# Float64 pairs in buffers of their own, x sums in eighths, an exponential unit in timed steps: a fused attention, expert and two-layer kernel

## The chip, the cores and the metric

One core of a Trainium2 chip runs the whole kernel. The metric is device time in microseconds (us). The engines are PE (TensorE: matmuls into PSUM), DVE (VectorE), ACT (ScalarE), POOL (GpSimd) and SP (SyncE), whose queue issues every DMA of this kernel, one after the other. Each engine runs its own instructions in the order in which the program emitted them; semaphores, placed by the tile framework, make an instruction wait for what it reads or overwrites.

## The reference

```python
attn = attention(q_l, k_l, v_l, q_g, k_g, v_g)        # 4 x 8 heads, 512 local (window 32) + 32 global rows
x = attn as 2176 rows of 512
P = exp(x @ w_gate - max); 8 times: rows, then columns of P divided by their sums     # 8 experts
x = sum over e of P[:, e] * (relu(x @ w1[e]) @ w2[e])   # w1: 512 x 1024, w2: 1024 x 512
h = x @ w_in                                            # 512 x 2048, float64 weights
g = where(h > 0, h, exp(min(h, 0)) - 1)                 # the exponential unit
out = g @ w_out                                         # 2048 x 512, float64 weights
```

## The kernel before, in words

Products are made in float32 accuracy: each operand is split into a high part hi (fp32r, a cast on ACT) and the remainder lo (a subtraction), and each product is three matmuls, hi x hi, hi x lo and lo x hi (`three`). The first layer of an expert or of the last network is computed with seven block products instead of eight (x and w in 2 x 2 blocks: sums t1 to t4 of w, s1 to s4 of x); `Quad.product(i)` makes one of them and, after it, `keep` (a partial sum s1, u2 or u3 in a `tmp` tile of that name, two buffers each) or `evac` (the result: the sum on DVE, then the activation into hh and hl, the two parts of the hidden layer in `hs`).

The stages follow each other: attention with the first two units in its gaps; then the MoE in two passes over the rows (pass 0: 1024 rows, 512-column products; pass 1: 1152 rows, 288-column products), 16 units of 512 hidden columns each; then the last network, called the second pass here, in 16 turns (turns 0 to 7 are its first 1024 rows, 8 to 15 the others, a tail ends them). `order` lists the MoE units from the third on: its units 0 to 13 are pass 0, 14 to 29 pass 1. A unit is `mix1` (first layer, two or four quads) and `mix2_all` (second layer: 8 or 9 tiles of 128 rows, each 12 matmuls into one PSUM bank, then `acc` on DVE).

All other work of the MoE stage is put between these steps by two lists of functions, written out by hand. `side1` is emptied in `mix1`, some functions after each product; `side2` in `mix2_all`, some after each tile. `None` in a list is a step in which nothing is emitted. In `side1` stand the loads of the next unit's w1 (w1r), the split of w2 into `w2s`, and the loads of other work; in `side2` the build of the next unit's w1 parts (`b1`: sums on POOL, hi on ACT, lo on DVE), `between` and `end` (other work) and the load of w2 (w2r). Loads go into four rotating `raw` tiles; a load waits until the tile's last use is over, and SP's later DMAs wait behind it.

The other work, by unit:
- `PAIRS`: `weights64_pair`. Two chunks of w_in (float64) are loaded; `words` takes the float32 value from the bits in six DVE instructions, with its results in ct and cp, which use the tags u2 and u3; `value` adds the rest (ACT, POOL). Then the four sums, hi and lo of seven blocks, in four further raw tiles, and 14 stores of 128 KB into scratch memory.
- singles (`weights64`): one chunk of w_out each, with hi and lo in `tmp` tiles (ch, cl) and two stores.
- `BACK`: `x_back`, the transposes of the first rows of the MoE's result.
- `OPERANDS`: `x_operands(2, c)`, two of four chunks of x: load, four sums on DVE (xsr), hi on ACT, lo on DVE, four stores; the chunks of the other rows (p = 3) run in turns 3 to 6.

In the second pass the order of a turn is a string: `a1` is product 1 of the turn's quad, `z3` product 3 of the quad before, `t4` the second layer's tile 4 (`part2`). `elu` computes the unit as max(t, 0) plus (e + 1) times the tanh of half of min(t, 0), with e its exponential: ACT makes three functions (relu, exp, tanh: tiles er and eg), DVE two instructions (the join, L1036 and L1037), ACT the cast hh, POOL the subtraction hl. What follows the three functions is a closure in `late`, which `rests()` runs at the next `elu` or at the end of the next `part2`. `passed(ns)` counts PE's work in `clock["now"]`; it served the gate's normalization only (`sinkhorn`).

Of the kernel before, what the change touches and what calls it, by code (L numbers as in the profile page):

```python
# [11 lines left out]
F32 = mybir.dt.float32  # L12
# [40 lines left out]
TURN_A = "a1 a6 t4 a2 t5 z3 t6 a7 t7 a5 t0 a4 t1 t2 t3"  # L53
# [8 lines left out]
def tile_net(ctx: ExitStack, tc, kq, vw, vc, qg, wg, w1, w2, wi, wo, consts, out):  # L62
# [721 lines left out]
    class Chunk:  # L784
# [9 lines left out]
        def words(self):  # L794
            top = self.r[:, :, 1]
            t = self.t = tmp.tile([128, 512], F32, tag="u2", name="ct")
            p = self.p = tmp.tile([128, 512], F32, tag="u3", name="cp")
# [7 lines left out]
            nc.vector.tensor_scalar(pi, ti, -2**23, None, op0=ALU.bitwise_and)  # L805

# [9 lines left out]
    def weights64(u, k):  # L816

        c = Chunk(wo[u, :, k])

        def parts():  # L820
            t = c.t
            hi = tmp.tile([128, 512], F32R, tag="s1", name="ch", bufs=2)
            lo = tmp.tile([128, 512], F32R, tag="cl", name="cl", bufs=1)
# [61 lines left out]
    def x_operands(p, c):  # L885

        k, g = divmod(c, 2)
        m = TP[p - 2] // 4
        s = {}

        def load():
            s["x"] = raw_tile((4, m), F32, "xr")
# [4 lines left out]
        def sums():  # L897
            x11, x21, x12, x22 = (s["x"][:, i] for i in range(4))
            t = s["s"] = raw_tile((4, m), F32, "xsr")
            s1, s2, s3, s4 = (t[:, i] for i in range(4))  # L900
            for o, a, b, op in (
                (s1, x21, x22, ALU.add), (s3, x11, x21, ALU.subtract), (s2, s1, x11, ALU.subtract), (s4, x12, s2, ALU.subtract),
            ):
                nc.vector.tensor_tensor(out=o, in0=a, in1=b, op=op)

        def hi(n):
            s[n + "h"] = raw_tile((4, m), F32R, "xh")
            nc.scalar.copy(s[n + "h"], s[n])

        def lo(n):  # L910
            nc.vector.tensor_tensor(out=s[n].bitcast(F32R), in0=s[n], in1=s[n + "h"].bitcast(F32), op=ALU.subtract)
            o = 0 if n == "x" else 4
            for q, t in (("h", s[n + "h"].bitcast(F32)), ("l", s[n])):
                nc.sync.dma_start(xo[p, q][:, o:o + 4, k, g * m:(g + 1) * m], t)

        return load, [sums, lambda: hi("x"), lambda: hi("s"), lambda: lo("x"), lambda: lo("s")]
# [18 lines left out]
    def sinkhorn():  # L935
# [62 lines left out]
    late = deque()  # L998
# [5 lines left out]
    class Quad:  # L1004
# [21 lines left out]
        def elu(self, hh, hl, t):  # L1026

            r = tmp.tile([128, 512], F32, tag="cl", name="er", bufs=1)[:, :self.n]
# [121 lines left out]
    with tc.manual_schedule():  # L1150
# [21 lines left out]
        back = {}  # L1172
# [99 lines left out]
        for k in range(len(turns) + 1):  # L1272
# [15 lines left out]
            for e in seq:  # L1288
# [8 lines left out]
                else:  # L1297
# [4 lines left out]
                    if i == 4 and q is quads[-1]:  # L1302
                        renew(k, W22[:-1])
# [79 lines left out]
```

## Time and profile before

| | us |
|---|---|
| median of 3 runs | 2113.37 (2111.77 to 2116.02) |
| the profiled execution | 2116.6 |
| its span, first to last instruction | 2114.8 |
| PE busy | 2020.4 |
| DVE busy | 1504.0 |
| ACT busy | 829.9 |
| POOL busy | 751.5 |
| mean granted TensorE clock | 0.981 |

The span is what the trace covers; the profiled execution's own time has 1.8 us around it. A granted clock of 1 is 2.4 GHz, 0.5 is 1.2 GHz. A windows row gives a stretch's length, then busy us and instruction count of PE, PEld (weight loads), DVE, ACT and POOL, the granted clock, the DMA engines' busy share and GB/s. Timeline rows are start, duration, engine, line, operation, out<-in and, in brackets, the engine's idle time before it with what ended it.

### The profile page before, as it was taken

The numbers are of one execution on the slowest core, as the hardware profiler recorded it, in microseconds if no ns is written. First come the engines' busy times: TensorE is split into PE (matmuls) and PEld (weight loads), VectorE is DVE, ScalarE is ACT, GpSimd is POOL, SyncE is SP. The second block draws the span as 40 slices with busy tenths as digits, with TensorE's granted clock in tenths as the row PEclk, the third lists the DMA queues.
The fourth block names the chain that finished last, engine by engine and source line by source line (L and its number), as shares of the span: only waits on it lengthen the run. The fifth ranks groups of instructions, "written<-read, shape, count | busy, mean of one in ns | idle before, by whom it ended". The sixth has DMA issues, their size and how long they took to land. (4 is left out here: it accounts for less than half of the span.)

```text
span 2114.8 us, 30653 instructions
## 1 busy us (share of the span) xinstructions
PE 2020.4 (96%) x11099; PEld 1740.5 (82%) x11099; DVE 1504.0 (71%) x2833; ACT 829.9 (39%) x1672; POOL 751.5 (36%) x649
## 2 busy tenths in 40 slices
PE   9999999999999999999999999999999998899998
PEld 8998888888888877798888888988889876678776
DVE  7767676677767777667676777878888566666666
ACT  6655424233233333333333333333333254445554
POOL 6656322233223355224242424444444121222221
PEclk9999999999999999999999999999999999899999
DMA  7446351132232233822324243232232945664321
GB/s 233 132 132 211 90 203 50 54 112 72 97 110 83 82 95 95 311 90 87 98 85 146 88 150 95 80 95 80 85 110 85 278 148 188 193 226 122 109 90 65
DMA packets 201047, 262.16 MB, mean 124 GB/s; under 512 B 13760, under 2 KB 147136, under 8 KB 200896
## 3 DMA queue, kind: packets, MB, share of 16 engines
q1 hardware_dynamic: 200896, 260.21, 38.6%
q8 instruction: 87, 1.43, 0.3%
q14 instruction: 64, 0.52, 0.1%
HBM read 194.62 MB, written 65.54 MB: 123 GB/s over the span
## 5 line engine op out<-in xcount | busy, mean ns | idle before, releaser
L133 PE MATMUL m<-w2h,hh 128*128 128x512 f32 x1360 | 542.6, 399 | 30.4 <-ACT hh L1038 24.9
L137 PE MATMUL m<-w2h,hl 128*128 128x512 f32 x1360 | 542.3, 399 | 15.2 <-POOL hl L1039 10.8
L135 PE MATMUL m<-w2l,hh 128*128 128x512 f32 x1360 | 539.1, 396 | 1.5 <-POOL w2l L129 1.5
L1020 ACT ACTIVATE hh<-t 128x288 fp32r<-128x288 f32 (+1 forms) x368 | 184.7, 502 | 432.1 <-DVE t L1014 429.5
L133 PEld LDWEIGHTS m<-w2h,hh 128*128 128x128 f32 x1360 | 259.2, 191 | 89.3 <-ACT hh L1038 34.1
L137 PEld LDWEIGHTS m<-w2h,hl 128*128 128x128 f32 x1360 | 258.6, 190 | 81.5 <-POOL hl L1039 24.3
L135 PEld LDWEIGHTS m<-w2l,hh 128*128 128x128 f32 x1360 | 259.0, 190 | 53.3 <-POOL w2l L129 4.2
L129 POOL TENSOR_TENSOR w2l<-w2r,w2h 128x512 fp32r<-128x512 f32 x120 | 163.0, 1380 | 388.9 <-ACT w2h L125 374.1
L1022 DVE SCALAR_TENSOR_TENSOR hl<-t,hh 128x288 fp32r<-128x288 f32 (+1 forms) x368 | 274.4, 746 | 28.0 <-ACT hh L1020 24.4
L1108 DVE SCALAR_TENSOR_TENSOR acc<-m,pr,acc 128x512 f32<-128x512 f32 x247 | 182.8, 745 | 117.9 <-PE m L137 116.5
L1039 POOL TENSOR_TENSOR hl<-eg,hh 128x288 fp32r<-128x288 f32 (+1 forms) x96 | 94.3, 982 | 362.7 <-ACT hh L1038 269.6
L1014 DVE TENSOR_TENSOR t<-q,u 128x288 f32<-128x288 f32 (+1 forms) x348 | 182.9, 526 | 52.3 <-PE q L1067 44.4
L741 POOL TENSOR_TENSOR wt<-w1r,wt 128x512 f32<-128x512 f32 x60 | 88.0, 1467 | 180.1 <-DVE hl L1022 94.3
L745 ACT CAST wh<-wt 128x512 fp32r<-128x512 f32 x120 | 69.9, 618 | 206.9 <-POOL wt L741 206.9
L741 POOL TENSOR_TENSOR wt<-w1r 128x512 f32<-128x512 f32 x60 | 79.8, 1334 | 181.4 <-DVE hl L1022 133.9
L1048 DVE TENSOR_TENSOR u<-q,s 128x288 f32<-128x288 f32 (+1 forms) x116 | 61.2, 528 | 98.0 <-PE q L1067 50.8
L749 DVE TENSOR_TENSOR wl<-wt,wh 128x512 fp32r<-128x512 f32 x120 | 121.8, 1032 | 2.2 <-ACT wh L745 1.0
L1036 DVE SCALAR_TENSOR_TENSOR eg<-eg,er 128x288 f32<-128x288 f32 (+1 forms) x96 | 51.7, 538 | 95.2 <-ACT er L1032 95.1
L1046 ACT COPY s<-q 128x288 f32<-128x288 f32 (+1 forms) x116 | 51.9, 448 | 114.6 <-PE q L1067 93.8
L1038 ACT CAST hh<-eg 128x288 fp32r<-128x288 f32 (+1 forms) x96 | 47.5, 495 | 117.8 <-DVE eg L1037 117.8
L810 POOL TENSOR_TENSOR cp<-r,cp 128x512 f32<-128x512 f32 x32 | 48.4, 1511 | 127.4 <-ACT r L809 78.3
L1249 DVE TENSOR_TENSOR acc<-m,acc 128x512 f32<-128x512 f32 x119 | 80.6, 683 | 17.3 <-PE m L137 17.3
(241 smaller groups left out, 4760.7 us busy)
## 6 DMA issues: line engine op xcount, KB each, us to landing
w1r<-in_w_dram SPq DMA_DIRECT2D x60, 512.0 KB, 6.4
w2r<-in_w_dram SPq DMA_DIRECT2D x60, 512.0 KB, 5.3
kq<-in_kq_dram SPq DMA_DIRECT2D x31, 544.0 KB, 4.2
wh<-wqh SPq DMA_DIRECT2D x98, 128.0 KB, 3.0
wl<-wql SPq DMA_DIRECT2D x98, 128.0 KB, 2.9
r<-in_wo_dram SPq DMA_DIRECT2D x16, 512.0 KB, 4.0
r<-in_wi_dram SPq DMA_DIRECT2D x16, 512.0 KB, 3.9
vw<-in_vw_dram SPq DMA_DIRECT2D x32, 227.5 KB, 4.7
```

Of the source, the lines that this page charges most:

```text
L129: e.tensor_tensor(out=lo, in0=src, in1=hi.bitcast(F32), op=ALU.subtract)
L133: nc.tensor.matmul(ps, ah, bh, start=first, stop=False)
L135: nc.tensor.matmul(ps, ah, bl, start=False, stop=False)
L137: nc.tensor.matmul(ps, al, bh, start=False, stop=last)
L741: eng.tensor_tensor(out=t, in0=get(a), in1=get(b), op=op)
L749: eng.tensor_tensor(out=wop[n + "l"], in0=src, in1=wop[n + "h"].bitcast(F32), op=ALU.subtract)
L1014: nc.vector.tensor_tensor(out=t, in0=ps, in1=rest, op=ALU.add)
L1020: nc.scalar.activation(hh, t, AF.Relu)
L1022: late.append(lambda: nc.vector.scalar_tensor_tensor(out=hl, in0=t, scalar=0.0, in1=hh.bitcast(F32), op0=ALU.max, op1=ALU.subtract))
L1039: nc.gpsimd.tensor_tensor(out=hl, in0=g, in1=hh.bitcast(F32), op=ALU.subtract)
L1108: nc.vector.scalar_tensor_tensor(out=accs[i], in0=ps, scalar=scale, in1=accs[i], op0=ALU.mult, op1=ALU.add)
L1249: nc.vector.tensor_tensor(out=accs[i], in0=ps, in1=accs[i], op=ALU.add)
```

## The change

- `PAIRS` move from units 10, 11, 12, 15, 17, 19, 21, 23 to 16, 18, 20, 22, 24, 26, 27, 28. Singles stand one each in units 1, 2, 4, 6, 8, 10, 11, 12, and two each in 17, 19, 21, 23 (before: one in 2, 4, 6, 8; two in 22 and 24 to 28). `BACK` is 14 and 15.
- ct and cp use the tags eg and cl, two buffers each. A pair's further results go into its two loaded tiles (`room`), into ct and into cp, and no longer into four raw tiles; its lo's move to POOL. Sums stand inside `b1`, the first casts (`plain`) in `end`; `hi`, `lo` and `store` become `later`, the first functions of the next unit's `side1`. A single's hi goes into its loaded tile, after `rest`, its lo into cp.
- x chunks become eight of half the width, sums in the loaded tile, lo on POOL, two stores. In pass 1 they stand in units 17, 19, 21, 23 (one each) and 25 (four). From unit 16 on `side2` is b1, end, between, w2r loads; before it was b1, between, w2r loads, end. In the second pass the loads are emitted one turn ahead (turns 2 to 5), the rest in turns 3 to 6.
- `elu` puts a join and a parts step into `stages`, due 1700 + 1.8 n ns and a further 500 + 1.5 n ns of counted PE time later (n columns); each is run after the first product or tile at which the clock is there, or at an `elu` that finds two units open. `part2` counts its matmuls. t0 stands behind a4 in `TURN_A`.

```diff
-BACK = (14, 16)
-OPERANDS = (18, 20)
-PAIRS = (10, 11, 12, 15, 17, 19, 21, 23)
+BACK = (14, 15)
+OPERANDS = {17: 1, 19: 1, 21: 1, 23: 1, 25: 4}
+PAIRS = (16, 18, 20, 22, 24, 26, 27, 28)
-TURN_A = "a1 a6 t4 a2 t5 z3 t6 a7 t7 a5 t0 a4 t1 t2 t3"
+TURN_A = "a1 a6 t4 a2 t5 z3 t6 a7 t7 a5 a4 t0 t1 t2 t3"
...
-            t = self.t = tmp.tile([128, 512], F32, tag="u2", name="ct")
-            p = self.p = tmp.tile([128, 512], F32, tag="u3", name="cp")
+            t = self.t = tmp.tile([128, 512], F32, tag="eg", name="ct", bufs=2)
+            p = self.p = tmp.tile([128, 512], F32, tag="cl", name="cp", bufs=2)
...
+        def room(self, dt, n=1):
+            r = self.r.rearrange("p f w -> p (f w)").bitcast(dt)
+            return r.rearrange("p (a f) -> p a f", a=n)
...
         def parts():
-            nc.scalar.copy(hi, t)
             c.rest()
-            nc.gpsimd.tensor_tensor(out=t, in0=t, in1=hi.bitcast(F32), op=ALU.subtract)
-            nc.gpsimd.tensor_tensor(out=lo, in0=t, in1=c.p, op=ALU.add)
+            hi = c.room(F32R, 2)[:, 0]
+            nc.scalar.copy(hi, c.t)
+            nc.gpsimd.tensor_tensor(out=c.t, in0=c.t, in1=hi.bitcast(F32), op=ALU.subtract)
+            nc.gpsimd.tensor_tensor(out=c.p.bitcast(F32R), in0=c.t, in1=c.p, op=ALU.add)
...
         def plain():
+            nc.scalar.copy(c1.p.bitcast(F32R), c1.t)
+            nc.scalar.copy(c0.p[:, :256].bitcast(F32R), blk("11"))
         def hi():
+            nc.scalar.copy(c1.room(F32R, 4), c0.room(F32, 4))
         def lo():
+            for t, h in ((c1.t, c1.p), (blk("11"), c0.p[:, :256]), (c0.room(F32, 4), c1.room(F32, 4))):
+                nc.gpsimd.tensor_tensor(out=t.bitcast(F32R), in0=t, in1=h, op=ALU.subtract)
...
     def x_operands(p, c):
-        k, g = divmod(c, 2)
-        m = TP[p - 2] // 4
+        k, g = divmod(c, 4)
+        m = TP[p - 2] // 8
...
+        def lo(o):
+            x, h = s["x"][:, o:o + 4], s["h"][:, o:o + 4]
+            nc.gpsimd.tensor_tensor(out=x.bitcast(F32R), in0=x, in1=h.bitcast(F32), op=ALU.subtract)
+            if o:
+                for q, t in (("h", s["h"].bitcast(F32)), ("l", s["x"])):
+                    nc.sync.dma_start(xo[p, q][:, :, k, g * m:(g + 1) * m], t)
+        return load, [first, lambda: hi(0), second, lambda: lo(0), lambda: hi(4), lambda: lo(4)]
...
         def elu(self, hh, hl, t):
+            while sum(e[2] for e in stages) > 1:
+                stages.pop(0)[1]()
             ...
-            rests()
-            late.append(rest)
+            wait = 1700.0 + self.n * 1.8
+            stages.extend([(clock["now"] + wait, join, 0), (clock["now"] + wait + 500.0 + self.n * 1.5, parts, 1)])
+            stages.sort(key=lambda e: e[0])
...
             elif a in PAIRS:
-                lds, (w0, v0, w1_, v1), between = weights64_pair(*pairs.popleft())
+                lds, (w0, v0, w1_, v1), (*tail, lo, store) = weights64_pair(*pairs.popleft())
                 side1.extend(lds)
-                b1[17:17], b1[13:13], b1[9:9], b1[5:5] = [v1], [w1_], [v0], [w0]
+                b1[13:13], b1[11:11], b1[9:9], b1[6:6], b1[3:3] = [tail[0]], [v1], [w1_], [v0], [w0]
+                end, later = tail[1:2], [tail[2], lo, store]
...
+            for _ in range(OPERANDS.get(a, 0)):
+                ld, ops = chunks2.popleft()
+                between += [ld, None, None, None] + ops
...
-            side2.extend(b1 + between + ld2 + end)
+            side2.extend(b1 + end + between + ld2 if a > BACK[-1] else b1 + between + ld2 + end)
...
-                    pass
+                    passed(227.0)
...
-            if 3 <= k < 7:
-                ld, ops = x_operands(3, k - 3)
-                ops = [ld, None, None] + ops
+            if k == 2:
+                work = [x_operands(3, c) for c in range(8)]
+                ops = [None] * 8
+            elif 3 <= k < 7:
+                ops = work[2 * k - 6][1] + work[2 * k - 5][1]
+            if 2 <= k < 6:
+                ops += [work[2 * k - 4][0], work[2 * k - 3][0]]
...
+                while stages and clock["now"] >= stages[0][0]:
+                    stages.pop(0)[1]()
```

## Rows read from the trace of the kernel before

**Rows 1.** the page: busy us of each engine, its share, its instructions.
```profile
PE 2020.4 (96%) x11099; PEld 1740.5 (82%) x11099; DVE 1504.0 (71%) x2833; ACT 829.9 (39%) x1672; POOL 751.5 (36%) x649
```

**Rows 2.** windows of pass 0 (stretch, length, busy us, clock): units 10, 11-13.
```profile
704.30:745.20 40.90, 40.90 (x181) 33.75 (x180) 30.32 (x43) 13.20 (x23) 16.38 (x12) 1.00 0.24 78
745.20:886.80 141.60, 132.64 (x541) 105.41 (x540) 100.34 (x137) 44.58 (x79) 67.52 (x54) 0.94 0.50 170
```

**Rows 3.** windows of pass 1: units 15, 16, 18, 19, 20 to 24.
```profile
935.50:982.30 46.80, 46.80 (x278) 42.53 (x277) 38.40 (x67) 16.43 (x36) 18.39 (x13) 1.00 0.17 59
982.30:1037.50 55.20, 50.57 (x293) 45.32 (x292) 32.30 (x59) 17.30 (x37) 16.19 (x15) 0.97 0.39 118
1084.30:1138.30 54.00, 49.32 (x278) 44.22 (x277) 34.76 (x63) 17.21 (x35) 16.57 (x15) 0.97 0.37 119
1138.30:1189.10 50.80, 47.38 (x277) 42.60 (x276) 41.90 (x75) 18.26 (x38) 18.72 (x13) 1.00 0.37 118
1189.10:1446.00 256.90, 244.09 (x1382) 220.07 (x1382) 196.89 (x343) 87.18 (x181) 102.98 (x80) 0.97 0.35 111
```

**Rows 4.** windows of the second pass: turns 0-1, 2, 3-6, 7, 8 on.
```profile
1680.00:1719.90 39.90, 36.19 (x164) 29.29 (x163) 24.19 (x33) 22.22 (x38) 9.07 (x7) 0.91 0.59 175
1719.90:1742.00 22.10, 21.26 (x92) 16.72 (x91) 12.50 (x19) 10.37 (x17) 3.87 (x3) 1.00 0.55 166
1742.00:1856.60 114.60, 96.40 (x361) 73.27 (x360) 75.09 (x112) 49.72 (x76) 21.81 (x16) 0.90 0.61 191
1856.60:1880.20 23.60, 21.92 (x92) 16.60 (x91) 14.37 (x22) 11.12 (x19) 5.27 (x5) 1.00 0.93 334
1880.20:2110.60 230.40, 212.60 (x1159) 179.45 (x1157) 147.88 (x310) 120.61 (x278) 54.28 (x66) 0.99 0.32 99
```

**Rows 5.** waits of DVE in unit 11: total us, times, longest.
```profile
DVE u L1048 <- issue: 5.7, 1, 5.7
```

**Rows 6.** timeline of SP, unit 16: start, us, engine, line, operation.
```profile
985.73 1.43 SPq L870 DMA_DIRECT2D wqh<-wth  x3
...
994.58 0.97 SPq L778 DMA_DIRECT2D w2r<-in_w_dram  x2
```

**Rows 7.** timeline of ACT, unit 16 (in brackets the idle time before).
```profile
999.63 0.62 ACT L125 CAST w2h<-w2r 128x512 fp32r<-128x512 f32 x1 [5.94 <-DMA w2r<-in_w_dram]
```

**Rows 8.** timeline of SP at the end of unit 18.
```profile
1134.37 0.88 SPq L914 DMA_DIRECT2D xo2l<-xsr  x1
1135.36 2.54 SPq L895 DMA_DIRECT2D xr<-xe  x2
```

**Rows 9.** timeline of DVE around the end of unit 18.
```profile
1141.66 0.76 DVE L904 TENSOR_TENSOR xsr<-xr 128x256 f32<-128x256 f32 x2 [7.32 <-DMA xr<-xe]
...
1147.38 0.45 DVE L1048 TENSOR_TENSOR u<-q,s 128x288 f32<-128x288 f32 x1
```

**Rows 10.** waits of all engines from 1680 us on.
```profile
DVE eg L1036 <- ACT er L1032: 95.1, 80, 2.5
...
PE m L133 <- ACT hh L1038: 24.9, 22, 4.2
...
PE m L137 <- POOL hl L1039: 10.8, 25, 1.0
```

**Rows 11.** timeline of DVE in turn 4.
```profile
1779.40 0.83 DVE L904 TENSOR_TENSOR xsr<-xr 128x288 f32<-128x288 f32 x2 [3.06 <-DMA xr<-xe]
```

**Rows 12.** timeline of POOL at the end of unit 24.
```profile
1443.61 1.51 POOL L810 TENSOR_TENSOR cp<-r,cp 128x512 f32<-128x512 f32 x1 [3.18 <-ACT r L809]
1445.09 1.74 POOL L826 TENSOR_TENSOR ct<-ct,ch 128x512 f32<-128x512 f32 x1
1446.92 1.62 POOL L827 TENSOR_TENSOR cl<-ct,cp 128x512 fp32r<-128x512 f32 x1
```

**Rows 13.** timeline of DVE at the end of unit 24.
```profile
1442.28 0.43 DVE L805 TENSOR_SCALAR cp<-ct 128x512 int32<-128x512 int32 x1
```

**Rows 14.** groups of ACT, turns 0 to 7: count, busy us, mean ns.
```profile
L1031 ACT ACTIVATE eg<-er 128x512 f32<-128x512 f32 x31 | 19.6, 632 | 3.6 <-POOL hl L1039 1.0
```

**Rows 15.** timeline of DVE in unit 16.
```profile
1003.02 1.59 DVE L1022 SCALAR_TENSOR_TENSOR hl<-t,hh 128x288 fp32r<-128x288 f32 x1
...
1007.64 0.45 DVE L1022 SCALAR_TENSOR_TENSOR hl<-t,hh 128x288 fp32r<-128x288 f32 x1
```

**Rows 16.** timeline of POOL in unit 16.
```profile
1000.33 5.42 POOL L129 TENSOR_TENSOR w2l<-w2r,w2h 128x512 fp32r<-128x512 f32 x4 [12.65 <-ACT w2h L125]
```

More of the change, by code (lines that the diff above doesn't have):

```diff
@@ L841, in sums @@
         def sums():
-            t = s["t"] = raw_tile((4, 256), F32, "wt")
-            t1, t3, t4, t2 = (t[:, i] for i in range(4))
+            t1, t3, t4, t2 = (c0.room(F32, 4)[:, i] for i in range(4))
             for o, a, b in (
@@ L895, in load, with comb, first, second @@
                 nc.sync.dma_start(s["x"][:, 2 * a:2 * a + 2], src[:, k, a, :, g * m:(g + 1) * m])
[L897 to L916, printed above, removed]
+        def comb(o, a, b, op):
+            x = s["x"]
+            nc.vector.tensor_tensor(out=x[:, o], in0=x[:, a], in1=x[:, b], op=op)
+        def first():
+            comb(4, 1, 3, ALU.add)
+            comb(6, 0, 1, ALU.subtract)
+        def second():
+            comb(5, 4, 0, ALU.subtract)
+            comb(7, 2, 5, ALU.subtract)
+        def hi(o):
+            if o == 0:
+                s["h"] = raw_tile((8, m), F32R, "xh")
+            nc.scalar.copy(s["h"][:, o:o + 4], s["x"][:, o:o + 4])
+        def lo(o):
[5 more added lines that the diff above has]
+        return load, [first, lambda: hi(0), second, lambda: lo(0), lambda: hi(4), lambda: lo(4)]
     def operands(p, names, c0, c1):
@@ L941, in gmax @@
             nc.vector.tensor_reduce(out=mx, in_=lg.rearrange("p t e -> p (t e)"), axis=AX.X, op=ALU.max)
-            mb = sm.tile([128, 128], F32, tag="mb", name="mb")
+            mb = tmp.tile([128, 512], F32, tag="t", name="mb", bufs=3)[:, :128]
             nc.vector.tensor_copy(mb, mx.to_broadcast([128, 128]))
@@ L996, in passed @@
                 clock["due"] = clock["now"] + timed[0][0]
-    late = deque()
+    late, stages = deque(), []
     def rests():
@@ L1171, in tile_net @@
         singles = deque((u, k) for u in range(U2) for k in range(4))
-        back = {}
+        chunks2 = deque(x_operands(2, c) for c in range(8))
+        back, later = {}, []
         def load_back(j):
@@ L1186, in tile_net @@
             b1, ld2, load2 = [], [], nbuild
+            side1.extend(later)
+            later = []
             if moe:
@@ L1199, in tile_net @@
                 between = [lambda i=i: x_back(i) for i in range(2 * j, 2 * j + 4)]
-            elif a in OPERANDS:
-                lds, ops = zip(*(x_operands(2, 2 * OPERANDS.index(a) + c) for c in range(2)))
-                side1.append(lds[0])
-                between = [*ops[0], lds[1], *ops[1]]
             elif a in PAIRS:
-                lds, (w0, v0, w1_, v1), between = weights64_pair(*pairs.popleft())
+                lds, (w0, v0, w1_, v1), (*tail, lo, store) = weights64_pair(*pairs.popleft())
                 side1.extend(lds)
-                b1[17:17], b1[13:13], b1[9:9], b1[5:5] = [v1], [w1_], [v0], [w0]
-            elif not switch and a > 1 and singles:
-                if a < BACK[0]:
-                    ld, end = weights64(*singles.popleft())
-                    side1.append(ld)
-                else:
-                    (l0, (c0, d0)), (l1, (c1, d1)) = (weights64(*singles.popleft()) for _ in range(2))
-                    side1.extend([l0, l1])
-                    b1[13:13], b1[9:9], b1[5:5] = [c1], [d0], [c0]
-                    end = [d1]
+                b1[13:13], b1[11:11], b1[9:9], b1[6:6], b1[3:3] = [tail[0]], [v1], [w1_], [v0], [w0]
+                end, later = tail[1:2], [tail[2], lo, store]
+            elif a > 0 and not switch and len(singles) > 8:
+                ld, end = weights64(*singles.popleft())
+                side1.append(ld)
+            elif a > BACK[-1] and singles and OPERANDS.get(a) == 1:
+                (l0, (c0, d0)), (l1, (c1, d1)) = (weights64(*singles.popleft()) for _ in range(2))
+                side1.extend([l0, l1])
+                b1[13:13], b1[9:9], b1[5:5] = [c1], [d0], [c0]
+                end = [d1]
+            for _ in range(OPERANDS.get(a, 0)):
+                ld, ops = chunks2.popleft()
+                between += [ld, None, None, None] + ops
             if not moe:
@@ L1307, in tile_net @@
             prev = quads[-1] if quads else None
-        rests()
     mright.close()
```

34 lines of the change are left out of this document (8 added, 26 removed).

## The prediction

> **What bounds the kernel now.** I read the page's busy shares first: PE is busy 96% of the span, DVE, the busiest of the engines beside it, 71% [rows 1]. So what can be won is PE's idle time and its slow stretches, and the question is where they lie. The windows view tells, cut where a unit begins (the first product with x11 after a run of mix2 matmuls; unit a is the a-th of `order`). In pass 0 a clean unit takes 40.9 us, so its 180 matmuls of 512 columns stand 0.227 us apart. Pairs are built in units 10, 11 and 12, and the units 11 to 13 behind them take 141.6 us, 18.9 over three clean ones, at a granted clock of 0.94 [rows 2]. In pass 1 a clean unit takes 46.8 us (a 288-column matmul: (46.8 - 108 x 0.227) / 168 = 0.133). Seven units are longer: 16, 18, 20, 22 and 24, each behind a pair, and 19 and 21, each behind two operand chunks. With 23, which is clean, they make 16 and 18 to 24. These take 55.2 + 54.0 + 50.8 + 256.9 us, 42.5 over eight clean ones [rows 3]; 0.9 of it are the 16 transposes of unit 16 (a quarter of 0.227 each), so 41.6 can go: 4.0 in unit 19, as much taken for unit 21, and 33.6 behind pairs. The second pass (from 1680 us) needs 28.6 + 2.0 us for turns 0 and 1 (126 matmuls, 36 transposes), 90 x 0.227 = 20.4 for each of turns 2 to 7, and 672 x 0.133 + 486 x 0.227 = 199.5 for the rest. It takes 39.9, 22.1, 114.6 (turns 3 to 6), 23.6 and 230.4: over by 9.3, 1.7, 33.0, 3.2 and 30.9, together 78.1 [rows 4]. So 18.9 + 41.6 + 78.1 = 138.6 us can go.
>
> The waits then say why. Behind a pair in pass 0, DVE waits 5.7 us at `keep`, where u2 shares its two buffers with the pair's ct [rows 5]. In pass 1 the pair's 14 stores hold SP's queue for 8.8 us and w2r is issued behind them [rows 6]; ACT stands 5.94 us before the cast of w2r, with every relu behind it [rows 7]. Behind chunks, the load of the second is issued behind the stores of the first [rows 8], and DVE stands 7.32 us before its sums [rows 9]. In the second pass PE waits 24.9 us for hh and 10.8 for hl, and behind that is DVE's order: it stands 95.1 us in 80 places before the first instruction of the join for ACT's tanh, with the next t's and acc's queued behind [rows 10], and in turns 3 to 6 also for the x load, 3.06 us in one [rows 11].
>
> **The change, part by part** (each sum against the profiled execution, 2116.6 us, which is 3.2 above the median of 2113.4).
>
> *Pass 0 without pairs: -18.9.* Units 10 to 12 get a single each, as units 2 to 8 had. The new single keeps hi in the loaded tile, so ACT's copy now waits for POOL's multiplication of 1.5 us [rows 12]; it stands at the end of mix2, where ACT has nothing for PE. ct and cp no longer take u2 and u3. Bounds: 0 to 1 us lost per single.
>
> *Pairs in pass 1: -33.6 + 1.* w2r is now loaded before the stores, which move into mix1 of the next unit; there they stand before w1r, needed half a unit later. POOL does the pair's lo there, which slows DVE's hl (below); 0 to 1 us per pair, I take 1 for all eight.
>
> *One chunk behind two singles, units 17, 19, 21, 23: +22.* Here I see a new wait: the load of x follows the second single's stores on SP. Take unit 24, which has two singles and ends at 1446.0. The second single's words end at 1442.7 on DVE [rows 13]; multiplication 1.5, ACT's copy 0.6 (a cast of 512 columns, [rows 7]), subtraction 1.7 and addition 1.6 follow [rows 12], later still by what ACT's new waits cost DVE (0 to 2 us). So the load is issued 3 to 4 us after the unit's end; its two issues take 2.5 [rows 8] and the landing 3.8 (1137.9 to 1141.66), less perhaps for half the bytes. DVE would stand before the sums until about 8 us after the end, with two acc's and the next u2 behind it, at about +11. In unit 18, which ends at 1138.3, the sums came at +3.4 and u2 at +9.1 [rows 9], and the loss was 4.0. I take 5.5 per unit; ends 2 and 9 (w2r is loaded last there and may stop ACT as in [rows 7]).
>
> *Unit 25, four chunks in a row: +20.* Chunk 0 is loaded early, in mix1. Each later load stands behind the stores of the chunk before. One round is 6.4 us from the last store's issue to the sums [rows 8, 9], then sums 1.1, a cast 0.6, lo on POOL twice 1.4 (one of them beside the cast) and stores 1.0: about 11. So the sums of chunks 1, 2 and 3 come at about +1, +12 and +23 us from the end of mix2, and the acc's of tiles 6, 7 and 8 stand between them on DVE. PE has five PSUM banks left (five products of 0.8 us), then waits: 23 + 4 to clear DVE, less 6.7 that it has to do, makes 20. Ends 8 and 25. The old chunks' 8.0 go. Pass 1 in sum: -33.6 + 1 + 22 + 20 - 8.0 = +1.4, say +2; by the ends -26 to +24.
>
> *The exponential unit in three steps: -59.* ACT's three functions take 3 x 0.63 us [rows 14]. The join is now issued 2.62 us after the product by PE's work (2.22 for 288 columns), when they have ended, and not at the next tile, where DVE stands 95.1 / 80 = 1.2 us for them [rows 10]; hi and lo follow 1.27 later (0.93). From turn 8 on DVE is busy 147.9 us [rows 4] where PE needs 199.5, so once nothing stands in DVE's queue PE waits for little. t0 moves behind a4, which gives z3's result one more product, 1.36 us. In turns 3 to 6 the load of x comes a turn early, so that stand goes as well, and lo moves from DVE to POOL. What is late next: a4's lo before t4 in turn 1, where ACT takes a2's three functions before a4's hi, 1.5 to 2 us. I leave 4 us in turns 0 and 1, then 1.3, 4 x 2 and 0.5, and 5 in the rest: 18.8 of 78.1. Ends 8 and 35 left: -70 to -43.
>
> *POOL beside DVE.* A hl of 0.45 us on DVE took 1.59 [rows 15] beside POOL's subtractions [rows 16]. With four lo's more on POOL in each of turns 3 to 6, 1.57 us each (5.42 / 4 x 576 / 512, rounded up), a join may be held each time: 0 to 6.3 us of DVE a turn. I take 2 of it on the path (above). The Trainium skill ("SBUF — State Buffer", Who interferes with whom) states that a DVE instruction with two SBUF inputs and a GpSimd instruction that reads SBUF exclude each other, whole instruction by whole instruction; the trace agrees with 1.59 for 0.45. By that rule all 6.3 us can land on DVE, which speaks against moving lo to POOL; what it gives is rival B.
>
> *At nothing:* the maximum's copy in a t buffer, which is read again within some us; the last pair's stores in unit 29, which builds no weights.
>
> Sum: -18.9 + 2 - 59 = -76: 2116.6 - 76 = 2040.6 for a profiled execution, 2037 for the median.
>
> **The rivals.**
> A. The loads of x are hidden after all: SP runs ahead, as it does for chunk 0. Units 17 to 25 then lose nothing: 2037 - 42 = 1995. Against it: the 7.32 us of [rows 9] come from the same order on SP. 15%.
> B. POOL's lo holds DVE in turns 3 to 6 for all 6.3 us: 4 x 4.3 = 17 more, 2054. For it: [rows 15]. Against it: DVE has room in a turn of 20.4. 10%.
> C. Slower: the steps come too late. They are issued only after a whole product or tile (1.36 us), so where PE already waits for hh, each of the 96 exponential units pays one step: 96 x 1.36 = 131 us in place of 78. -18.9 + 2 + 53 = +36, 2149; it ends above the time before from 0.99 us per unit on ((78.1 + 16.9) / 96). Against it: the tiles stand five or six steps behind the product that they need. 3%.
> D. The steps change little, since hh and hl are late by their own chain (t, three functions, join, hi, lo) and not by the order; only the x part of turns 3 to 6 goes (33.0 to about 10). -18.9 + 2 - 23 = -40: 2073. For it: PE's waits for hl come 25 times, at most 1.0 us each [rows 10]. 6%.
>
> **How the numbers follow.** My forecast has 65%; its own range is 2014 to 2060 (pass 1 between -18 and +18, the second pass between -66 and -48). 1% is left for a mixture that ends near the time before; about 0.2% (4 us) is what a measurement here tells from no change. The forecast, A, B and D are faster: 96%; C is slower: 3%; same 1%. The range of 8 in 10 takes in half of A and all of B: 2000 to 2064.
>
> **What would show it.** Right: units 11 to 13 at 41 us; the units behind pairs in pass 1 within 1 us of 46.8; units 18, 20, 22 and 24 long by 3 to 8 us, with DVE standing for the x load; unit 26 near 66 us; turns 3 to 6 at 22 to 23 us, and 204 to 205 us from turn 8 on, with DVE's stand before the join small. Wrong: no DMA wait of DVE in unit 25 (A), turns 3 to 6 over 26 us with DVE busy throughout (B), PE's waits for hh above 25 us in the second pass (C, D).

## The result, and the profile after

The changed kernel takes 2047.47 us (2047.24 to 2048.72) against 2114.69 (2111.77 to 2116.88) beside it: ratio 0.9684, interval 0.9667 to 0.9701. It is 67 us faster where 76 were forecast, inside the range of 2000 to 2064. The profiled spans are 2045.5 and 2114.8, so 69.3 us are to be found in the traces.

The page after: PE's busy time falls by 34.6 us only; the rest of the gain is idle time. POOL has 52 us more, DVE 16.

```profile
PE 1985.8 (97%) x11099; PEld 1729.0 (85%) x11099; DVE 1520.1 (74%) x2841; ACT 822.9 (40%) x1680; POOL 803.6 (39%) x681
```

The windows view after, columns as in [rows 2]: units 11 to 13; unit 17 (behind a pair); units 18 to 24; 26; then turns 0 and 1, 2, 3 to 6, 7, from 8 on.

```profile
745.50:868.40 122.90, 122.90 (x542) 101.34 (x541) 84.51 (x117) 38.82 (x68) 42.51 (x32) 1.00 0.42 147
1012.50:1059.30 46.80, 46.80 (x277) 42.54 (x276) 40.39 (x68) 17.75 (x36) 24.35 (x18) 1.00 0.36 108
1059.30:1404.60 345.30, 333.65 (x1934) 302.59 (x1933) 281.84 (x494) 122.45 (x256) 168.51 (x124) 0.99 0.35 108
1451.40:1515.30 63.90, 50.78 (x277) 45.73 (x276) 41.61 (x81) 19.57 (x41) 26.57 (x21) 0.87 0.37 115
1655.70:1694.90 39.20, 34.77 (x164) 28.21 (x163) 27.88 (x33) 21.11 (x37) 9.58 (x7) 0.96 0.58 171
1694.90:1715.70 20.80, 20.80 (x92) 16.83 (x91) 14.69 (x21) 10.78 (x18) 3.87 (x3) 1.00 0.80 236
1715.70:1815.20 99.50, 89.64 (x362) 68.74 (x361) 78.96 (x121) 50.41 (x84) 44.18 (x32) 0.97 0.68 202
1815.20:1836.60 21.40, 21.07 (x91) 16.70 (x90) 16.38 (x23) 10.22 (x17) 7.50 (x6) 1.00 0.99 360
1836.60:2041.20 204.60, 202.13 (x1158) 179.60 (x1158) 163.08 (x309) 114.30 (x277) 55.69 (x67) 1.00 0.38 118
```

Units 11 to 13 are clean (141.6 before, -18.7) [rows 2], and so is every unit behind a pair. Units 18 to 24 lose 17.7 us over seven clean ones of 46.8, unit 26 loses 17.1 [rows 3]; pass 1 gains 5.9 in all. The second pass goes from 434.8 to 389.8, -45.0 [rows 4]: from turn 8 on it does what the forecast says, but turns 0 and 1 gain 0.7 where 5.3 were forecast, and turns 3 to 6 gain 15.1 where 25 were. The attention is 0.3 us longer. -18.7 - 5.9 - 45.0 + 0.3 = -69.3.

The border between turns 6 and 7 is not the same in every execution: e1, e4 and e5 (below), whose second pass is that of the changed kernel, have 97.3 to 97.5 us in turns 3 to 6 and 23.1 in turn 7, where the windows above have 99.5 and 21.4. The sums differ by 0.5 at most.

SP, then DVE, behind unit 17, which ends at 1059.3 (answers [rows 8, 9]):

```profile
1061.45 0.32 SPq L832 DMA_DIRECT2D wdl<-cp  x1
1061.87 0.93 SPq L887 DMA_DIRECT2D xr<-xe  x2
```
```profile
1064.74 1.02 DVE L891 TENSOR_TENSOR xr<-xr 128x128 f32<-128x128 f32 x4 [3.81 <-DMA xr<-xe]
1065.68 1.40 DVE L1110 SCALAR_TENSOR_TENSOR acc<-m,pr,acc 128x512 f32<-128x512 f32 x2
1067.00 0.45 DVE L1050 TENSOR_TENSOR u<-q,s 128x288 f32<-128x288 f32 x1
```

The x load goes out behind the second single's store; DVE stands for it with two acc's and u2 queued behind. With the four chunks of unit 25 this comes three times (SP, then DVE; the rounds are 8.7 us apart), most of it in unit 26:

```profile
1454.77 0.52 SPq L911 DMA_DIRECT2D xo2l<-xr  x1
1455.33 1.83 SPq L887 DMA_DIRECT2D xr<-xe  x2
```
```profile
1451.04 1.02 DVE L891 TENSOR_TENSOR xr<-xr 128x128 f32<-128x128 f32 x4 [7.00 <-DMA xr<-xe]
1459.72 1.02 DVE L891 TENSOR_TENSOR xr<-xr 128x128 f32<-128x128 f32 x4 [6.99 <-DMA xr<-xe]
1468.38 0.49 DVE L891 TENSOR_TENSOR xr<-xr 128x128 f32<-128x128 f32 x2 [6.97 <-DMA xr<-xe]
```

Waits from turn 0 on (us, times, longest), against [rows 10]: DVE's stand before the join went from 95.1 us in 80 places to 8.3 in 9, PE's for hh from 24.9 to 9.6. The longest that is left for DVE, waits for PE aside, is the x load, 11.1 us in three places [rows 11].

```profile
DVE xr L891 <- DMA xr<-xe: 11.1, 3, 4.1
PE m L133 <- ACT hh L1038: 9.6, 7, 3.7
DVE eg L1034 <- ACT er L1031: 8.3, 9, 1.0
PE m L137 <- POOL hl L1039: 7.3, 13, 1.0
```

ACT in turn 1: the three functions of a2 stand ahead of the hh (1674.86) for which PE stands 3.7 us.

```profile
1672.94 0.63 ACT L1029 ACTIVATE er<-t 128x512 f32<-128x512 f32 x1 [3.28 <-DVE t L1011]
...
1674.86 0.60 ACT L1038 CAST hh<-eg 128x512 fp32r<-128x512 f32 x1
```

POOL, SP and DVE at the start of turn 4 (1737.5): hl queues behind lo, and the x loads go out behind the store that waits for the same lo. So DVE gets x 7.5 us into the turn.

```profile
1738.40 1.46 POOL L908 TENSOR_TENSOR xr<-xr,xh 128x576 fp32r<-128x576 f32 x1 [3.69 <-ACT xh L904]
1739.82 2.95 POOL L1039 TENSOR_TENSOR hl<-eg,hh 128x512 fp32r<-128x512 f32 x2
```
```profile
1739.89 0.52 SPq L911 DMA_DIRECT2D xo3l<-xr  x1
1740.46 3.11 SPq L887 DMA_DIRECT2D xr<-xe  x4
```
```profile
1738.61 1.80 DVE L1035 SCALAR_TENSOR_TENSOR eg<-t,eg 128x512 f32<-128x512 f32 x1
...
1745.05 0.53 DVE L891 TENSOR_TENSOR xr<-xr 128x144 f32<-128x144 f32 x2 [3.44 <-DMA xr<-xe]
```

### The profile page after: what moved, and what is told of

Read it like the earlier page. It is cut to its first block, busy times and chain, and to the rows that moved or that the text cites. A ratio compares the mean times of both kernels' runs of the same rounds, so it can differ in the third digit from the quotient of the medians.

```text
span 2045.5 us, 30595 instructions
## 1 busy us (share of the span) xinstructions
PE 1985.8 (97%) x11099; PEld 1729.0 (85%) x11099; DVE 1520.1 (74%) x2841; ACT 822.9 (40%) x1680; POOL 803.6 (39%) x681
## 5 line engine op out<-in xcount | busy, mean ns | idle before, releaser
L133 PE MATMUL m<-w2h,hh 128*128 128x512 f32 x1360 | 536.0, 394 | 9.8 <-ACT hh L1038 9.6
L137 PE MATMUL m<-w2h,hl 128*128 128x512 f32 x1360 | 536.9, 395 | 7.3 <-POOL hl L1039 7.3
L1019 DVE SCALAR_TENSOR_TENSOR hl<-t,hh 128x288 fp32r<-128x288 f32 (+1 forms) x368 | 279.9, 761 | 13.2 <-ACT hh L1017 9.5
L749 DVE TENSOR_TENSOR wl<-wt,wh 128x512 fp32r<-128x512 f32 x120 | 115.0, 969 | 13.5 <-ACT wh L745 11.6
L1067 PE MATMUL q<-x11h,wh 128*128 128x288 f32 (+1 forms) x232 | 76.5, 330 | 17.0 <-DVE acc L1110 17.0
L255 ACT ACTIVATE e<-s,m 128x192 f32<-128x192 f32 (+1 forms) x128 | 55.7, 436 | 79.8 <-DVE m L247 79.2
```

What stands on the lines that cost most here:

```text
L133: nc.tensor.matmul(ps, ah, bh, start=first, stop=False)
L137: nc.tensor.matmul(ps, al, bh, start=False, stop=last)
L749: eng.tensor_tensor(out=wop[n + "l"], in0=src, in1=wop[n + "h"].bitcast(F32), op=ALU.subtract)
L1019: late.append(lambda: nc.vector.scalar_tensor_tensor(out=hl, in0=t, scalar=0.0, in1=hh.bitcast(F32), op0=ALU.max, op1=ALU.subtract))
L1067: nc.tensor.matmul(ps, wh, xh, start=k == 0 and i != 3, stop=False, skip_group_check=True)
```

## The experiments

Each is the changed kernel with one edit (e5, e8, e9 and e11 hold several, as named), timed beside the kernel before (2115.6 to 2115.8 us). Stretches are lengths of the windows view; `...` in an edit marks lines left out.

**e1, x loads of pass 1 early** (two in `b1`, the others one chunk ahead).
```diff
-            for _ in range(OPERANDS.get(a, 0)):
-                ld, ops = chunks2.popleft()
-                between += [ld, None, None, None] + ops
+            chunks = [chunks2.popleft() for _ in range(OPERANDS.get(a, 0))]
+            b1[5:5] = [c[0] for c in chunks[:2]]
+            for i, (_, ops) in enumerate(chunks):
+                between += ops + [c[0] for c in chunks[i + 2:i + 3]]
```


> Changed kernel with one thing moved: in pass 1 the load of an x chunk is issued on SP ahead of the two singles' stores (units 17, 19, 21, 23), and in unit 25 the loads of chunks 0 and 1 come first, those of 2 and 3 one chunk ahead. Order theory (DVE stands for a load that SP holds behind stores): units 18, 20, 22, 24 go from 50.5 to 52.6 us back to 46.8 to 47.5, unit 26 from 63.9 to 47 to 50, so 28 to 34 us less, 2013 to 2019 us. Rival (the work of a chunk itself overloads DVE or POOL there): at most 8 us less, 2039 us or more.

Measured: 2023.0 us (2021.47 to 2024.63), ratio 0.9553 (0.9525 to 0.9580). Units 18 to 24:
```profile
1059.30:1393.10 333.80, 328.90 (x1933) 297.87 (x1932) 283.20 (x494) 121.61 (x255) 168.55 (x124) 1.00 0.36 111
```
They fall from 345.3 to 333.8, unit 26 from 63.9 to 49.7: 25.7 us of the 34.8 lost there were the place of the load on SP's queue. The gain of 24.5 us is short of the 28 to 34 expected. ACT's waits show what is late next: w2r, issued at 1066.21 behind the chunk's last store.
```profile
ACT w2h L125 <- DMA w2r<-in_w_dram: 12.9, 4, 4.5
```

**e2, x lo of turns 3 to 6 on DVE** instead of POOL.
```diff
-            nc.gpsimd.tensor_tensor(out=x.bitcast(F32R), in0=x, in1=h.bitcast(F32), op=ALU.subtract)
+            e = nc.vector if p == 3 else nc.gpsimd
+            e.tensor_tensor(out=x.bitcast(F32R), in0=x, in1=h.bitcast(F32), op=ALU.subtract)
```


> Changed kernel with the lo of the x chunks of the second pass (turns 3 to 6) back on DVE. Shared-path theory (POOL's lo holds the joins on DVE and stands before hl on POOL): turns 3 to 6, 99.5 us in the changed kernel, go to 90 to 94, 6 to 9 us less in all, 2038 to 2042 us. Rival (DVE has no room, or the late x load sets these turns): the same or up to 5 us more, 2046 to 2053 us.

Measured: 2050.28 us (2047.41 to 2052.56), ratio 0.9681 (0.9652 to 0.971). Turns 3 to 6, and 7:
```profile
1716.60:1815.70 99.10, 90.32 (x362) 69.79 (x361) 81.92 (x133) 48.86 (x82) 20.45 (x16) 0.95 0.68 202
1815.70:1840.90 25.20, 22.71 (x92) 17.64 (x91) 18.39 (x26) 11.51 (x20) 6.54 (x5) 0.93 0.94 350
```
Nothing is won in 3 to 6 (99.5) and 3.8 us are lost in 7 (21.4); together they are 3.4 to 3.9 longer than in the changed kernel, e1, e4 and e5. Here half of the joins are short (median of the second join 693 ns, 1661 in the changed kernel), but joins and hl's are still late, now behind lo on DVE. So the place of lo on POOL does not by itself explain these turns. DVE still stands 7.3 us for the x load here, so what lo costs on either engine when the load comes in time is not shown.

**e3, the exponential unit in its old order** (`late` and `rests()`, old `TURN_A`; everything else as changed).
```diff
-TURN_A = "a1 a6 t4 a2 t5 z3 t6 a7 t7 a5 a4 t0 t1 t2 t3"
+TURN_A = "a1 a6 t4 a2 t5 z3 t6 a7 t7 a5 t0 a4 t1 t2 t3"
...
-            stages.extend([(clock["now"] + wait, join, 0), (clock["now"] + wait + 500.0 + self.n * 1.5, parts, 1)])
-            stages.sort(key=lambda e: e[0])
+            late.append(rest)
...
+            rests()
```


> Changed kernel with the exponential unit issued as before (the rest of a unit at the next unit or tile) and the old place of t0; pairs, singles and x chunks stay as changed. Steps theory: from turn 8 on 204.6 us become 228 to 231, turns 0 to 7 lose 5 to 15 more, so 28 to 42 us slower than the changed kernel, 2075 to 2090 us. Rival (the second pass gained by the earlier x loads and not by the steps): at most 10 us slower, 2057 us or less.

Measured: 2073.82 us (2071.9 to 2074.7), ratio 0.9791 (0.9763 to 0.982). Turns 0 and 1, 3 to 6, from 8 on:
```profile
1655.50:1691.60 36.10, 33.56 (x163) 27.15 (x162) 24.48 (x33) 21.39 (x37) 9.63 (x7) 1.00 0.61 185
1713.70:1817.30 103.60, 89.97 (x362) 68.72 (x361) 66.41 (x120) 50.66 (x85) 42.55 (x32) 0.97 0.65 194
1840.30:2065.90 225.60, 211.21 (x1159) 179.74 (x1157) 147.48 (x310) 118.09 (x278) 54.36 (x66) 0.99 0.33 103
```
The three steps, with the place of t0, are worth 26.3 us, less than the 28 to 42 expected: 21.0 from turn 8 on, 4.1 in turns 3 to 6, and in turns 0 and 1 they cost 3.1. From turn 8 on 4.8 of the 25.8 us won [rows 4] stay without them; `er` has two buffers in the changed kernel and in e3 where it had one before, which may be why, but no run takes that away alone.

**e4, pairs back in pass 0** (units 10 to 12), in their new form; the singles change places with them.
```diff
-PAIRS = (16, 18, 20, 22, 24, 26, 27, 28)
+PAIRS = (10, 11, 12, 16, 18, 20, 22, 24)
...
-            elif a > 0 and not switch and len(singles) > 8:
+            elif a > 0 and not switch and len(singles) > 10:
...
```


> Changed kernel with three pairs back in units 10, 11 and 12 (the others in 16, 18, 20, 22, 24), in their new buffers and with the new order of the build; five singles in units 1 to 8, the rest two each in 19, 21, 23, 26, 27 and one in 17. Buffer theory (u2 and u3 and the raw tiles made the loss in pass 0, not the place): units 11 to 13 take 41.0 to 41.5 us each, 46.7 to 47.5 before, and the whole is within 4 us of the changed kernel, 2043 to 2051 us. Rival (a pair cannot stand in a 41 us unit): units 11 to 13 lose 3 us or more each, 2056 us or more.

Measured: 2046.6 us (2046.15 to 2047.21), ratio 0.9663 (0.9631 to 0.9696). Units 11 to 13:
```profile
746.40:869.30 122.90, 122.90 (x541) 101.36 (x540) 100.09 (x133) 44.88 (x78) 72.15 (x54) 1.00 0.55 184
```
With the pairs beside them they are as clean as without: the 18.9 us of [rows 2] came from the old form of the pairs and not from their place. The trace before tells which part of it. In unit 11, POOL (the last read of ct), SP, ACT and DVE:
```profile
749.85 3.11 POOL L855 TENSOR_TENSOR wpl<-ct,wph 128x256 fp32r<-128x256 f32 x3
```
```profile
757.90 0.48 SPq L870 DMA_DIRECT2D wql<-wt  x1
758.43 0.97 SPq L778 DMA_DIRECT2D w2r<-in_w_dram  x2
```
```profile
762.97 0.62 ACT L125 CAST w2h<-w2r 128x512 fp32r<-128x512 f32 x1 [4.48 <-DMA w2r<-in_w_dram]
763.50 0.58 ACT L1046 COPY s<-q 128x512 f32<-128x512 f32 x1
```
```profile
764.16 0.69 DVE L1048 TENSOR_TENSOR u<-q,s 128x512 f32<-128x512 f32 x1 [5.74 <-issue]
```
ct was read for the last time 11 us before, so DVE's 5.7 us of [rows 5] were no wait for a buffer: u2 reads s1, which ACT copied by 764.08, behind the cast of w2r, and w2r was issued behind the pair's 14 stores. That is the chain of [rows 6] and [rows 7] again; units 12 and 13 show the same, with DVE standing 6.5 and 6.4 us. In e4 the stores come after w2r, and ACT has no wait for it.

**e5, e1 with w2r ahead of the single's tail and the x work.**
```diff
-            side2.extend(b1 + end + between + ld2 if a > BACK[-1] else b1 + between + ld2 + end)
+            w2first = BACK[-1] < a and a != 25
+            side2.extend(b1 + ld2 + end + between if w2first else b1 + end + between + ld2 if a > BACK[-1] else b1 + between + ld2 + end)
```


> The kernel with the early x loads (e1), and in units 16 to 29 but 25 the loads of the second layer's weights (w2r) are also emitted ahead of the pair's or single's tail and the x work. My theory: the 0.98 to 1.22 us that TensorE still waits for xs4h in units 18, 20, 22 and 24 of e1 come from w2r standing on SP's queue behind the x work; with w2r first these units fall from 47.9, 49.6, 48.1 and 47.8 us to about 46.9 each, and the time by some 4 us, to 2017 to 2020. Rival: what is late there is ACT or DVE, which work on the x chunk whatever the order on SP; then the units stay at 47.8 or more and the time within 2 us of e1's 2023.

Measured: 2029.72 us (2028.91 to 2030.76), ratio 0.9592 (0.9576 to 0.9607): 6.7 slower than e1. Units 18 to 24 take 340.7 us. ACT's waits there:
```profile
ACT xh L904 <- DMA wdh<-r: 28.7, 4, 7.2
```
The wait for w2r is gone, but ACT stands 7.2 us in each long unit, for the single's store. The `raw` tiles rotate: with w2r first, xh is given the tile that holds the single's hi until its store has read it. Neither theory had this.

**e6, due stages ahead of the three functions.**
```diff
-            while sum(e[2] for e in stages) > 1:
+            while stages and (clock["now"] >= stages[0][0] or sum(e[2] for e in stages) > 1):
```


> The changed kernel, with one difference: stages that are due are emitted before the next unit's three functions, not after. My theory for turns 0 and 1 (39.2 us against a floor of 30.7, and 36.2 with the old unit order): in turn 1 ACT runs a2's three functions (2 us) ahead of a4's due copy to hh, and TensorE stands 3.95 us for it. With the due copy first, turns 0 and 1 fall to 35 to 36.5 us and the time to 2043 to 2045. Rival: DVE's joins and POOL's subtraction, which share their path to the buffers (joins of 1.65 to 1.80 us), are what comes last; then turns 0 and 1 stay over 38.5 us and the time within 1 us of 2047.5.

Measured: 2041.78 us (2041.04 to 2043.65), ratio 0.965 (0.9634 to 0.9666). Turns 0 and 1, then ACT in turn 1:
```profile
1653.10:1689.90 36.80, 34.92 (x164) 28.31 (x163) 24.51 (x33) 21.99 (x38) 9.02 (x7) 0.95 0.68 203
```
```profile
1669.68 0.62 ACT L1038 CAST hh<-eg 128x512 fp32r<-128x512 f32 x1 [2.68 <-DVE eg L1035]
```
hh now stands ahead of the three functions (the first starts at 1670.28), and PE's wait for it falls from 3.7 us to 1.2. The turns are 2.4 us shorter, slightly less than expected, and those from turn 8 on 0.8. Most of the rest of the 5.7 lies ahead of turn 0, where the edit changes nothing: unit 26 alone takes 62.3 to 63.9 us in the executions that leave pass 1 as it is.

**e7, loads of the second pass' x a chunk earlier** (ops, load, ops, load in place of ops, ops, load, load).
```diff
-                ops = work[2 * k - 6][1] + work[2 * k - 5][1]
+                ops = work[2 * k - 6][1] + [w[0] for w in work[2 * k - 4:2 * k - 3]] + work[2 * k - 5][1]
...
-                ops += [work[2 * k - 4][0], work[2 * k - 3][0]]
+                ops += [w[0] for w in work[2 * k - 4 + (k > 2):2 * k - 2]]
```


> The changed kernel, with one difference: in turns 3 to 6 the loads of the next x chunk stand right behind the first chunk's work of the turn (a chunk earlier), not behind both. My theory: at the start of turns 4, 5 and 6 DVE stands 3.4, 3.6 and 4.2 us for an x load that is issued behind the store of the chunk before; two thirds of these 11.1 us reach TensorE through the joins queued behind on DVE. Expected: DVE's wait for the x load under 1 us a turn, turns 3 to 6 from 99.5 us to 91 to 95, the time 2040 to 2043. Rival: POOL's lo and the joins that it stretches (1.81 us) set these turns; then DVE waits elsewhere instead, and turns 3 to 6 stay above 97.5 us.

Measured: 2044.12 us (2043.05 to 2045.6), ratio 0.9658 (0.9639 to 0.9676). Turns 3 to 6, and 7:
```profile
1718.30:1810.30 92.00, 85.28 (x361) 66.81 (x360) 78.26 (x119) 49.70 (x82) 43.61 (x31) 1.00 0.74 218
1810.30:1835.00 24.70, 23.06 (x92) 17.85 (x92) 18.12 (x25) 11.59 (x20) 8.35 (x6) 0.93 0.93 343
```
DVE no longer stands for x, and turns 3 to 6 lose 7.5 us, as expected; turn 7 gives 3.3 back, and the time misses its expectation by 1. Part of both is not the edit's doing. Turns 3 to 6, and 7, of e1, whose second pass is that of the changed kernel:
```profile
1690.40:1787.70 97.30, 87.96 (x361) 67.61 (x360) 77.34 (x119) 49.14 (x82) 43.74 (x31) 0.98 0.69 206
1787.70:1810.80 23.10, 21.47 (x91) 16.66 (x91) 18.04 (x25) 11.58 (x20) 8.28 (x6) 1.00 0.93 341
```
Against these, turns 3 to 6 lose 5.3 us. Turn 7 takes 24.7 us here at a granted clock of 0.93 and 23.1 at 1.00 in e1, and in e11 too, which has this edit. So these rows show no cost of the edit itself in turn 7; 1.6 us go with the clock.

**e8, e1, e5, e6 and e7 together.** Its diff is the four above.

> The four reorderings in one kernel: x loads of pass 1 early (e1), w2r first (e5), due stages first (e6), the second pass' x loads a chunk early (e7). If they are in different places and independent, the sum of their gains: e1 -24.5 (measured), e5 about -4, e6 about -3, e7 about -6: 2008 to 2014. Rival: the gains in the second pass overlap (the same joins on DVE are freed twice), so that e6 and e7 together bring at most 5 us: 2014 to 2017.

Measured: 2019.06 us (2015.9 to 2020.77), ratio 0.9539 (0.9521 to 0.9557), above both ranges, which had put e5 at a gain. Turns 0 and 1 take 35.2 us and turns 3 to 6 91.9, so e6 and e7 do add up; e5's part is a loss here too.

**e9, e1, e6 and e7 together**, w2r behind the x work again.

> Three of the four reorderings together: pass 1's x loads early (e1), due stages first (e6), the second pass' x loads a chunk early (e7); w2r stays behind the x work, as in the changed kernel. My theory: with w2r first, xh of the x chunk took the slot of the single's raw words, and waited 7.1 us for the single's stores (unit 18 of e5); without it units 18, 20, 22 and 24 are back at 47.9, 49.6, 48.1 and 47.8 us. From e1's 2023.0: e6 brought 5.7 and e7 3.4, so 2012 to 2016. Rival: units 18 to 24 stay at 49.4 us each as in e8, from another cause: then 2018 to 2020.

Measured: 2011.23 us (2010.75 to 2012.16), ratio 0.9507 (0.949 to 0.9523). Units 18, 20, 22 and 24 are back at 47.8, 49.4, 47.8 and 47.7: e5's loss is its order.

**e10, without the arithmetic on x in turns 3 to 6**: DVE's sums, xh and lo are left out, the chunk is stored as loaded.
```diff
+        def store():
+            for q, t in (("h", s["x"]), ("l", s["x"])):
...
+        if p == 3:
+            return load, [None, None, None, None, None, store]
```


> The changed kernel without the arithmetic on the second pass' x chunks in turns 3 to 6: DVE's sums, ACT's xh and POOL's lo are left out; the loads and the stores (as halves, twice as many) stay. Floor of these four turns 81.6 us (4 x 20.4), measured 99.5 in the changed kernel and 92.0 with the loads a chunk earlier (e7). My theory: nearly all of the loss in turns 3 to 6 is this arithmetic's place among the joins and hl, the exponential unit's three steps by themselves lose under 1 us a turn: turns 3 to 6 at 82 to 86 us, turn 7 at 20.5 to 21.5, the time 2029 to 2035. Rival: the timed steps lose 2 us a turn with or without x work, as the prediction had it; then turns 3 to 6 take 89 us or more and the time 2037 or more.

Measured: 2030.99 us (2029.56 to 2032.92), ratio 0.9597 (0.9577 to 0.9618). Turns 3 to 6:
```profile
1717.30:1801.30 84.00, 84.00 (x361) 66.94 (x360) 65.15 (x89) 40.91 (x68) 22.98 (x17) 1.00 0.88 253
```
The x arithmetic, with the stand for the load that goes along with it, is 15.5 of the 17.9 us that turns 3 to 6 stand over their floor of 81.6; the timed steps alone leave 0.6 a turn. The joins remain stretched (group of DVE's second join in these turns: ns lowest, median, highest), so the stretch by itself costs PE at most those 0.6:
```profile
L1042 DVE SCALAR_TENSOR_TENSOR eg<-t,eg x17: 691/1657/1672, 1716.8 to 1800.7; 128x512 f32<-128x512 f32 x17
```

**e11, e9 with w2r behind the chunk's first sums and first xh.**
```diff
+            if a > BACK[-1] and a != 25:
+                between[2:2] = ld2
+                ld2 = []
```


> e9 with one difference: in units 16 to 29 but 25 the w2r loads stand behind the x chunk's first sums and first xh, not behind all of its work (and not ahead of it, as in e5). Theory (slots): xh takes its slot before w2r does, so it does not wait for the single's stores as in e5, and w2r is issued some 3 us earlier than in e9: the 0.9 to 1.2 us waits for xs4h in units 18 to 24 go, 47.9, 49.6, 48.1 and 47.8 us become about 46.9 each, the time 3 to 5 us under e9's. Rival: w2r's own slot is one that frees late (the x chunk's or the single's), so SP's queue stands and the stores behind it too; then these units stay at 47.8 us or more, and the time is within 2 us of e9's or above it.

Measured: 2005.73 us (2003.65 to 2006.52), ratio 0.9479 (0.9461 to 0.9496): the fastest version, 42 us under the changed kernel and 5.5 under e9 (3 to 5 expected). Units 18 to 25, and SP behind unit 17:
```profile
1058.00:1432.40 374.40, 374.40 (x2209) 340.26 (x2208) 322.05 (x560) 139.48 (x291) 190.09 (x140) 1.00 0.38 114
```
```profile
1060.51 0.92 SPq L778 DMA_DIRECT2D w2r<-in_w_dram  x2
...
1064.37 0.52 SPq L911 DMA_DIRECT2D xo2l<-xr  x1
```
All eight are clean (8 x 46.8 = 374.4): w2r goes out 3.9 us ahead of the chunk's last store, xh has its tile before w2r takes one, and no wait for w2r is left. This settles pass 1 but for unit 26, which keeps 3.1 us.

## Why the prediction was right, and where its sizes were off

The sum is 7 us off because two larger misses went opposite ways, which is luck: pass 1 came out at -5.9 where +2 was forecast, and the second pass at -45.0 where -59 was, outside the -66 to -48 that the forecast's own range allowed for it. Of its signs, turns 3 to 6 at 22 to 23 us failed (24.9, and 24.3 to 24.4 in e1, e4 and e5); the others came. The upper end of pass 1, +24, is mis-added: the ends given make +27.

- *Pass 0, -18.9*: right (-18.7) for another reason than the one given. [rows 5] were read as a wait for u2's buffers, but ct was free 11 us before; DVE and PE stood for w2r behind the pair's stores, as in pass 1 (e4). Moving the pairs away took the stores away too; in their new form they could have stayed.
- *Pairs in pass 1, -33.6 + 1*: all eight units behind pairs are clean, so the 1 us for POOL's lo did not come. (Unit 21, taken as 4.0 over, was 5.4 over before; the 33.6 is 1.4 less by that, and the sum of 41.6 stays.)
- *One chunk behind two singles, +22*: right in mechanism and place, shown by e1; 17.7 was measured. "Until about 8 us after the end" was 5.4 (1064.74 - 1059.3): the load was issued 2.6 us after the unit's end and not 3 to 4, two half-size loads took 0.93 us of issue where I had 2.54 of [rows 8], and landed 1.9 us after it and not 3.8. Rival A is excluded.
- *Unit 25, +20*: right, 17.1, three rounds of 8.7 us where I had 11. Of the 17.1, 13.1 is PE idle (63.9 - 50.8) and 4.0 longer matmuls, at a mean granted clock of 0.87. With the old chunks' 8.0, pass 1 is -33.6 + 17.7 + 17.1 - 8.0 + 1.0 (unit 15, now an `x_back` unit of 48.7 us, is 1.9 over a clean one; 0.9 of it lay inside unit 16 before) = -5.8, against the +2 forecast.
- *Turns 0 and 1, "I leave 4 us"*: this term was mis-sized. The place was named (a2's three functions ahead of a4's hi), the price was 8.6 us over the floor of 30.6 in place of 4. PE's stand of 3.7 us at hh is one part of it, and e6 shows that it is the order on ACT. In e8, e9 and e11, which have that order too, the turns take 35.2 to 35.3 us at a clock of 1.00, where e6 has 36.8 at 0.95. The old unit order did better than the new (36.1, e3).
- *Turns 3 to 6, "the load of x comes a turn early, so that stand goes as well"*: this step failed, and it is the largest miss (17.9 us left where 8 were forecast; 15.7 to 15.9 in e1, e4 and e5). The load is emitted a turn early, but SP issues in order, and it stands behind a store that waits for the last lo on POOL. DVE stood 11.1 us. With the load a chunk earlier (e7) 10.4 us are left, and without x arithmetic (e10) 2.4. The 8.0 between them (92.0 - 84.0) equal the 4 x 2 put for POOL's lo by luck: they hold DVE's sums and ACT's casts as well, and no run leaves out lo alone. (A lo took 1.46 us; the 1.57 of the sum is 1.52 by its own rows.) A held join is not the way it costs: e10 has the long joins, beside hl, and loses 0.6 us a turn, and e2 loses as much with lo on DVE. By the rows of turn 4 and by e2 it is x work queued ahead of a join or of hl, on either engine.
- *Turn 2, turn 7, from turn 8 on*: 20.8, 21.4 (23.1 in e1, e4 and e5) and 204.6 us where 21.7, 20.9 and 204.5 were forecast; e3 shows that the steps did 21.0 of the 25.8 from turn 8 on. Rivals C and D are excluded: PE stands 9.6 us for hh, not above 25.
- *Rival B* points to the right turns for the wrong reason: without lo on POOL (e2) they are no shorter. By the Trainium skill ("SBUF — State Buffer", Who interferes with whom) a DVE instruction with two SBUF inputs and a GpSimd instruction that reads SBUF exclude each other. The trace agrees on durations, with a join of 1.80 us beside lo where others take 0.69. That such a join costs PE its full length, as the rival had it, is not borne out here.

Not settled: which part of the 4.6 us still left in turns 0 and 1 of e8 (35.2) is due to hl on POOL, and why the clock falls in turn 7 of e7 and not of e11 (turns 3 to 7 together take 115.1 us in e11, against 116.7 in e7).

## What to carry to other kernels

A load that is emitted early is only early if nothing ahead of it on its in-order queue waits for late work: read the start times of SP's rows and not the place in the program. Moving a load also moves its claim on a rotating tile, so check who gets the tile that frees last (e8 against e11, which differ in the place of w2r alone: 13 us). Before a wait is put down to a buffer, look up when that buffer was last read, and what the instruction's inputs waited for. When an order on engines is changed by due times, issue what is due before the next long group, and price the turns where the new order starts by themselves, since there it can be worse than the old.

## What was not expected of the hardware

PE's idle time costs more than itself. Unit 26 is 17.1 us long for 13.1 us of idle; the rest is longer matmuls. PE stood there until 1461.6 and again until 1469.6, 6.1 and 6.3 us, and the granted clock was 0.50 (1.2 GHz) in this stretch:

```profile
1458.00:1475.10 17.10, 7.29 (x29) 6.97 (x30) 7.47 (x21) 4.39 (x9) 5.03 (x4) 0.50 0.47 142
```

Turns 3 to 6 of the changed kernel take 15.5 us more than in e10 for 9.9 of idle. The longer matmuls lie in turns 4 and 6, at a clock of 0.94 (2.5 us of PE's busy time each over e10's 21.0), and less in 3 and 5, at 1.00 (0.1 and 0.6).

Two issues of half-size x loads took 0.93 us behind unit 17 and 1.83 in unit 26, where full-size ones took 2.54 [rows 8]; why they differ among themselves no run tells.
